# Phase tables as matrix products in the set-up of an FFT-and-feed-forward kernel, with the first batch folded in two halves

## The chip, the cores and the metric

The kernel runs on one core of one Trainium2 chip. The core has five engines with queues of their own: TensorE (PE; its weight loads are listed as PEld), VectorE (DVE), ScalarE (ACT), GpSimd (POOL) and SyncE (SP). The metric is device time in microseconds of one execution, and the median of several runs is compared. The profile is one execution taken by the hardware profiler. All times inside it are counted from the start of its span.

## The reference

The input x has 8 batches of 3008 rows of 256 numbers. A Fourier transform runs over both axes of each batch and its real part is kept. Every row of 256 then goes through a feed-forward layer with a squared ReLU.

```python
X = np.fft.fft(np.fft.fft(x, axis=1), axis=2).real      # 8 x 3008 x 256
h = np.maximum(X.reshape(24064, 256) @ w_in, 0.0)       # w_in 256 x 2048
out = h * h @ w_out                                     # w_out 2048 x 256
```

## The kernel before

All heavy work is matmuls in 16 bits with sums in 32 bits. The transform is done by products with cosine and sine tables, and symmetry makes the products small. A row of x and its mirror image are added and subtracted ("folded"), along the 256 columns (`fe`, `fo`) and then along the 3008 rows (`ab`). The result is split again into odd and even output frequencies. For the odd class the folded tile is `od`, with part 0 for cosines and part 1 for sines; its tables are `cos0` and `sin0`, six rows of 376 frequencies for each of the 128 partitions.

`z_steps` (L468) multiplies `od` with the tables. Each unit has parts 0 and 1 and halves h = 0 and 1, of three matmuls each (L488) into a PSUM tile `pz`. After half 0, ACT copies the partial sum to `es` (L493); after half 1, ACT copies the sum into the window's columns `zc` or `zs` (L497); the step `minus` (L504, on DVE) forms the mirrored columns as 2 es - ps.

The transform along the columns is merged into the input weights. `gh_step` (L440) multiplies the tables `c_all` and `s_n` with a quarter of w_in (512 of 2048 columns) in PSUM, and its `scale` step writes the quarter into `gh`, rows 0 and 1, by ACT or DVE. `gh_turn` (L456) makes row 2 from row 1 with the factors `turn2`. So for each window of z columns the hidden values are gh[0] times zc plus gh[1] times zs; adding gh[2] times zs then gives those of the mirrored columns.

The loop over windows w (L697) makes the hidden values, squares them into `h2`, and multiplies the h2 of the window before with the output weights `wout16` (L628). Windows 0 and 1 have 240 and 512 columns. Window 0 takes two groups of four steps: `pq4` (eight matmuls, L834 and L835), `square4` (ACT's relu L844, DVE's square L847), `turn4` (four matmuls, L840), and `square4` again. `others(s)` issues what is planned beside step s. Window 1 carries the fold of the second batch (`x1`), with DVE work in `d_even`, `n_cos`, `d_odd`, `n_sin` and `odds`, then `nyq`, two tiny matmuls on PE (L383, L384) and a DVE copy (L385).

The order on each engine is the order in which the program issues it; no scheduler reorders it. DMAs of the inputs are issued by POOL. `load_x` (L124 on) loads a batch in one direct transfer (L133: the first two quarters of the rows) and two gathers through index vectors (L138: the mirrored quarters). The order on POOL is: iotas `nvec_i`, `irow_i`, `dvec_i`, `idx_r`; load of the first batch; iota `prow_i` and two permutation matrices `perm`; two small index vectors; the two halves of w_in (`w16`, L185); w_out (L187). The load of the second batch is issued in `d_odd` and waits for the DVE instruction that last reads the first batch.

The odd tables are made by `table_steps(0)`. The phase n times k modulo 3008 comes out of elementwise work: six ACT instructions `args` (L240) that round n k / 3008 to a whole number, `turns` (L246) and `mods` (L252) on DVE, then two sines over 1128 columns (L258). Row 1 gets a weight (L279). The cosines are the sines of mirrored rows, fetched by matmuls with the permutations (L268) and copied by ACT (L269). The tables for the columns are made in a like way on ACT and DVE (L294 to L322). `idle(n)` (L308) issues n matmuls of 384 columns on zeros, whose results nobody reads.

PSUM pools: `ps_h`, two tiles of 2 x 512; `ps_o` and `ps_z`, two tiles of 512 each. `h1p` has five tiles, used in turn by the relus.

Of the kernel before, what the change touches and what calls it, by code (L numbers as in the profile page):

```python
# [15 lines left out]
P = 128  # L16
# [12 lines left out]
def kernel(  # L29
# [94 lines left out]
    def load_x(i):  # L124
# [18 lines left out]

        if b > 0:
            direct(0, 2)
        else:
# [5 lines left out]
        gather(2, idx["r" if b + 1 < B else "c"][:, 0:1], o + (S - R * (P - 1)) * D)  # L152
# [5 lines left out]
        gather(3, idx["r"][:, 0:1], o + (H - R * (P - 1)) * D)  # L158
        return t

    def iota(shape, pattern, base, mult, name):
        t = const.tile(shape, I32, name=name)
        nc.gpsimd.iota(t, pattern=pattern, base=base, channel_multiplier=mult)
        return t
# [3 lines left out]
    nvec_i = iota([P, R], [[1, R]], -5, R, "nvec_i")  # L168
    irow_i = iota([P, NE], [[1, NE]], 0, 0, "irow_i")
    dvec_i = iota([P, 2], [[P, 2]], 0, 1, "dvec_i")  # L170
# [6 lines left out]
    for i in (1, 0):  # L177
        nc.gpsimd.tensor_scalar(out=perm[i], in0=prow_i, scalar1=float(P - 1 - i), scalar2=None, op0=ALU.is_equal)
# [5 lines left out]
    for i in range(2):  # L184
        nc.gpsimd.dma_start(out=w16[i], in_=moe_w_in[:, i * F // 2 : (i + 1) * F // 2].rearrange("(c p) f -> p c f", p=P))  # L185
    wout16 = const.tile([P, NFC, D], F16, name="wout16")
# [9 lines left out]
    nraw = small([P, R], "nraw")  # L196
    nc.vector.tensor_copy(nraw, nvec_i)
    irow = small([P, NE], "irow")
    nc.vector.tensor_copy(irow, irow_i)

    nvec = small([P, R], "nvec")
    nc.vector.scalar_tensor_tensor(out=nvec, in0=nraw, scalar=float(Q), in1=nraw, op0=ALU.is_le, op1=ALU.mult)
    nc.vector.tensor_scalar(out=nvec, in0=nvec, scalar1=0.0, scalar2=None, op0=ALU.max)
    nvs = small([P, R], "nvs")
    nc.vector.tensor_scalar(out=nvs, in0=nvec, scalar1=1.0 / S, scalar2=None, op0=ALU.mult)

    wgt = small([P, 1], "wgt")
    nc.vector.tensor_scalar(out=wgt, in0=nraw[:, 1:2], scalar1=float(Q), scalar2=-0.5, op0=ALU.is_equal, op1=ALU.mult)
# [4 lines left out]
    def table_steps(e):  # L213

        n = unit_cols[e][0]
        nr = 2 if e else 3
        cos_t = const.tile([P, 2 if e else R, n], F16, name=f"cos{e}")
        sin_t = const.tile([P, 2 if e else R, n], F16, name=f"sin{e}")
        tabs[e] = (cos_t, sin_t)
        vec, vs = (evec, evs) if e else (nvec, nvs)  # L220
        st = {}

        def row(h, j):
            return j if e else RQ[3 * h + j]

        def freq():
            kf = st["kf"] = tmp.tile([P, NE], F32, name="kf", tag="kf")[:, 0:n]
            i = 0
            for k0, kstep, cnt in unit_runs[e][0]:
                nc.vector.tensor_scalar(out=kf[:, i : i + cnt], in0=irow[:, i : i + cnt], scalar1=float(kstep), scalar2=float(k0 - kstep * i), op0=ALU.mult, op1=ALU.add)  # L230
                i += cnt

        def args(h):
            tm = tmp.tile([P, 2, 3, NE], F32, name="tm", tag="tt")
            t, st["m", h] = tm[:, 0], tm[:, 1]
            st["t", h] = t
            for j in range(nr):
                r = row(h, j)
                if e == 0:
                    nc.scalar.activation(t[:, j, 0:n], st["kf"], AF.Copy, bias=R23, scale=vs[:, r : r + 1])  # L240
                else:
                    nc.vector.tensor_scalar(out=t[:, j, 0:n], in0=st["kf"], scalar1=vs[:, r : r + 1], scalar2=R23, op0=ALU.mult, op1=ALU.add)
# [5 lines left out]
        def mods(h):  # L248
            m = st["m", h]
            for j in range(nr):  # L250
                r = row(h, j)
                nc.vector.scalar_tensor_tensor(out=m[:, j, 0:n], in0=st["kf"], scalar=vec[:, r : r + 1], in1=st["t", h][:, j, 0:n], op0=ALU.mult, op1=ALU.add)  # L252
# [4 lines left out]
        def sins(h):  # L257
            nc.scalar.activation(sin_t[:, 3 * h : 3 * h + nr, :], st["m", h][:, 0:nr, 0:n], AF.Sin, bias=0.0, scale=wk)  # L258

        def coss(h):  # L260
            if e:
                nc.scalar.activation(cos_t, st["t", h][:, 0:nr, 0:n], AF.Sin, bias=halfpi[:, 0:1], scale=-wk)
                return

            pc = ps_h.tile([P, 2, 512], F32, name="pc", tag="psh")
            for j in range(2):
                r = RQ[2 * h + j]
                nc.tensor.matmul(pc[:, j, 0:n], perm[1 if r else 0], sin_t[:, RQ.index(6 - r if r else 0), :], start=True, stop=True)  # L268
            nc.scalar.activation(cos_t[:, 2 * h : 2 * h + 2, :], pc[:, :, 0:n], AF.Copy, bias=0.0, scale=1.0)  # L269

        def weigh():
            if e:
                for t in (cos_t, sin_t):
                    for r in range(2):
                        nc.vector.tensor_scalar(out=t[:, r, :], in0=t[:, r, :], scalar1=wge[:, r : r + 1], scalar2=None, op0=ALU.mult)
                return

            q = RQ.index(1)
            nc.scalar.activation(sin_t[:, q, :], sin_t[:, q, :], AF.Copy, bias=0.0, scale=wgt)  # L279
# [3 lines left out]
    to = table_steps(0)  # L283
    to["freq"]()

    dvec = small([P, 2], "dvec")
    nc.vector.tensor_copy(dvec, dvec_i)
    dvs = small([P, 2], "dvs")
    nc.vector.tensor_scalar(out=dvs, in0=dvec, scalar1=1.0 / D, scalar2=None, op0=ALU.mult)
    drow = irow[:, 0 : P + 1]  # L290
    am = h1p.tile([P, 2, P + 1], F32, name="am", tag="h1")
    at = h1p.tile([P, 2, P + 1], F32, name="at", tag="h1")
    for c in range(2):
        nc.scalar.activation(at[:, c, :], drow, AF.Copy, bias=R23, scale=dvs[:, c : c + 1])  # L294
    nc.vector.tensor_scalar(out=at, in0=at, scalar1=-R23, scalar2=-float(D), op0=ALU.add, op1=ALU.mult)
    for c in range(2):
        nc.vector.scalar_tensor_tensor(out=am[:, c, :], in0=drow, scalar=dvec[:, c : c + 1], in1=at[:, c, :], op0=ALU.mult, op1=ALU.add)
# [7 lines left out]
    nc.vector.memset(fe.rearrange("p q c d -> p (q c) d")[:, :, 129:130], 0.0)  # L305
    pw = ps_o.tile([P, 512], F32, name="pw", tag="po")
# [6 lines left out]
    idle(16)  # L313
    to["args"](0)
    to["args"](1)
    wd = 2.0 * math.pi / D
    s_n = const.tile([P, 2, P + 1], F16, name="s_n")
    nc.scalar.activation(s_n, am, AF.Sin, bias=0.0, scale=-wd)
    nc.vector.tensor_scalar(out=at.bitcast(I32), in0=am.bitcast(I32), scalar1=0x7FFFFFFF, scalar2=None, op0=ALU.bitwise_and)
    c_all = const.tile([P, 2, P + 1], F16, name="c_all")  # L320
    nc.scalar.activation(c_all, at, AF.Sin, bias=halfpi[:, 0:1], scale=-wd)
    nc.scalar.activation(s_n[:, :, 0:1], c_all[:, :, P : P + 1], AF.Copy, bias=0.0, scale=0.5)  # L322

    to["turns"](0)
    to["mods"](0)
    to["sins"](0)
    to["turns"](1)
    to["weigh"]()
    idle(4)
    to["coss"](0)  # L330
    to["mods"](1)
    to["sins"](1)
    idle(6)
    to["coss"](1)
    to["coss"](2)
    idle(4)

    turn2 = small([P, 1], "turn2")
    nc.vector.tensor_scalar(out=turn2, in0=dvec[:, 0:1], scalar1=0.0, scalar2=2.0, op0=ALU.is_equal, op1=ALU.mult)
    nc.vector.tensor_scalar(out=turn2, in0=turn2, scalar1=-2.0, scalar2=None, op0=ALU.add)  # L340
# [3 lines left out]
    def fold_steps(i):  # L344
# [7 lines left out]
        lo = xf[:, :, 1:129]  # L352
        hi = rev_dim(xf[:, :, 128:256], 2)
# [3 lines left out]
        def d_even():  # L357
            nc.vector.tensor_copy(t[0:1, 2, 0, :], t[0:1, 0, R - 1, :])
            nc.vector.tensor_tensor(fef[:, :, 1:129], lo, hi, op=ALU.add)
            nc.vector.tensor_copy(fef[:, :, 0:1], xf[:, :, 0:1])  # L360

        def d_odd():
            nc.vector.tensor_tensor(fof[:, :, 1:129], lo, hi, op=ALU.subtract)
            if i + 1 < B:
                xs[i + 1] = load_x(i + 1)

        def n_cos():
            nc.vector.tensor_tensor(ab[:, 0], fe[:, 0:2], rev_dim(fe[:, 2:4], 2), op=ALU.add)

        def n_sin():  # L370
            nc.vector.tensor_tensor(ab[:, 1], fo[:, 0:2], rev_dim(fo[:, 2:4], 2), op=ALU.subtract)
# [566 lines left out]
```

## Time and profile before

| What | us |
|---|---|
| median of 3 runs | 603.11 (601.97 to 604.74) |
| profiled execution, its own time | 604.8 |
| its span | 603.0 |
| mean granted TensorE clock | 0.997 of full |
| first matmul of window 0 (L834) | 23.40 |
| first relu of window 0 (L844) | 24.94 |
| first matmul of window 1 (L748) | 31.45 |
| fold of the second batch starts on DVE (L358) | 35.09 |

The profile's pages list for each engine how long it was busy, what ended its idle time, and the chain of work that ended last. A row of the timeline gives start, length, engine, line, operation, output and inputs, and in brackets the idle time ahead of it and what ended it. A count such as x6 is several like instructions merged in one row.

### The profile page before, as it was taken

How to read it: one execution, taken by the hardware profiler on the slowest of the kernel's cores; microseconds unless marked ns; L12 is line 12 of the kernel's file. 1: busy time of each engine (PE TensorE's matmuls, PEld its weight loads, DVE VectorE, ACT ScalarE, POOL GpSimd, SP SyncE). 2: the span in 40 equal slices, each digit the busy share in tenths (PEclk: the TensorE clock that was granted, in tenths of full speed). 3: DMA queues.
4: the chain of work that ended last, by engine and by line, in shares of the span. 5: the costliest groups of instructions: out<-in, count | busy, mean ns of one | idle time of the engine just before them, and what ended most of it. 6: DMA issues, size and time to landing. Idle time of an engine off the chain costs nothing.

```text
span 603.0 us, 11343 instructions
## 1 busy us (share of the span) xinstructions
PE 580.4 (96%) x4376; PEld 421.1 (70%) x4376; DVE 515.0 (85%) x740; ACT 515.4 (85%) x663; POOL 88.7 (15%) x125
## 2 busy tenths in 40 slices
PE   5899999999999999999999999999999999999997
PEld 2557776777677677777677766766777776776786
DVE  7797677887999988989989899888998699889981
ACT  7596788888999889989899898979989888888972
POOL 5353200103001032020012200401000020000000
PEclk9899999999999999999999999999999999999999
DMA  8937120273213533542154311643112231211222
GB/s 143 205 85 161 56 71 31 63 154 92 68 45 72 135 113 70 128 116 56 51 111 91 111 45 54 116 111 90 48 33 71 71 89 46 61 43 48 60 59 68
DMA packets 39736, 50.33 MB, mean 83 GB/s; under 512 B 4589, under 2 KB 33539, under 8 KB 39683
## 3 DMA queue, kind: packets, MB, share of 16 engines
q0 software_dynamic: 9344, 22.14, 18.6%
q1 hardware_dynamic: 26899, 24.44, 13.8%
q10 hardware_dynamic: 3440, 3.03, 2.1%
q8 instruction: 34, 0.56, 0.4%
q14 instruction: 19, 0.16, 0.1%
HBM read 36.42 MB, written 27.86 MB: 107 GB/s over the span
## 4 chain that ended last, share of the span: by engine, by line
PE 66%; ACT 12%; DVE 10%; issue 5%; DMA 4%; POOL 1%; ACTq 0%; SPq 0%; DVEq 0%; POOLq 0%
PE po L628 39%; PE ph L787 5%; PE ph L773 5%; PE ph L754 4%; PE ph L748 4%; ACT h L758 4%; PE ph L749 4%; PE pz L488 3%; ACT sn L781 3%; DMA out_dram<-osb 2%; ACT osb L643 2%; DVE h L813 2%; ACT hd L789 2%; DVE hd L812 2%; DVE hd L811 1%
## 5 line engine op out<-in xcount | busy, mean ns | idle before, releaser
L628 PE MATMUL po<-wout,h 128*128 128x256 f16 (+1 forms) x3024 | 362.0, 273 | 1.3 <-DVE h L813 1.3
L628 PEld LDWEIGHTS <-h 128*128 128x128 f16 (+1 forms) x3024 | 296.4, 98 | 73.0 <-DVE h L813 1.8
L758 ACT ACTIVATE h<-ph 128x1024 f16<-128x1024 f32 (+3 forms) x196 | 185.6, 981 | 13.8 <-PE ph L754 8.3
L763 DVE TENSOR_TENSOR h<-h 128x1024 f16<-128x1024 f16 (+3 forms) x135 | 85.3, 657 | 26.5 <-ACT h L758 25.2
L789 ACT ACTIVATE hd<-ph 128x1024 f16<-128x1024 f32 (+3 forms) x94 | 94.0, 1001 | 14.9 <-PE ph L787 13.4
L813 DVE TENSOR_TENSOR h<-hd 128x4096 f16<-128x4096 f16 (+6 forms) x51 | 105.4, 2066 | 1.4
L781 ACT ACTIVATE sn<-ph 128x1024 f16<-128x1024 f32 (+3 forms) x94 | 93.6, 996 | 1.0 <-PE ph L773 0.7
L643 ACT ACTIVATE osb<-po 128x512 f32<-128x512 f32 (+3 forms) x95 | 54.6, 578 | 24.8 <-PE po L628 24.0
L748 PE MATMUL ph<-zc,gh 128*128 128x512 f16 (+3 forms) x196 | 72.1, 368 | 0.5 <-ACT h L844 0.3
L749 PE MATMUL ph<-zs,gh 128*128 128x512 f16 (+3 forms) x196 | 72.1, 368 | 0.0
L797 DVE TENSOR_SCALAR hd<-eb,wv 128x512 f16<-128x512 f16 (+3 forms) x188 | 54.2, 348 | 15.1 <-DMA eb<-zr 15.1
L801 DVE TENSOR_TENSOR sn<-sn,hd 128x2048 f16<-128x2048 f16 (+6 forms) x51 | 56.7, 1113 | 11.8 <-ACT sn L781 8.1
L811 DVE TENSOR_TENSOR hd<-hd,sn 128x2048 f16<-128x2048 f16 (+6 forms) x51 | 56.6, 1111 | 9.8 <-ACT hd L789 8.4
L761 ACT ACTIVATE h<-h 128x1024 f16<-128x1024 f16 (+3 forms) x61 | 62.7, 1028 | 1.9
L787 PE MATMUL ph<-zc,gh 128*128 128x512 f16 (+3 forms) x188 | 54.6, 371 | 5.7 <-ACT sn L781 4.7
L812 DVE TENSOR_SCALAR hd<-hd 128x4096 f16<-128x4096 f16 (+6 forms) x51 | 56.8, 1114 | 1.5
L754 PE MATMUL ph<-zs,gh 128*128 128x512 f16 (+3 forms) x196 | 55.3, 368 | 0.2 <-ACT h L758 0.2
L773 PE MATMUL ph<-zs,gh 128*128 128x512 f16 (+3 forms) x188 | 54.5, 372 | 0.0
L749 PEld LDWEIGHTS <-gh 128*128 128x128 f16 x196 | 19.1, 98 | 21.2 <-issue 1.0
L748 PEld LDWEIGHTS <-gh 128*128 128x128 f16 x196 | 19.1, 97 | 20.3
L773 PEld LDWEIGHTS <-gh 128*128 128x128 f16 x188 | 18.3, 97 | 20.9
L787 PEld LDWEIGHTS <-gh 128*128 128x128 f16 x188 | 17.1, 97 | 13.7 <-issue 9.5
(129 smaller groups left out, 408.2 us busy)
## 6 DMA issues: line engine op xcount, KB each, us to landing
out_dram<-osb SPq DMA_DIRECT2D x77, 128.0 KB
xo<-in_x_dram POOLq DMA_DIRECT2D x7, 768.0 KB, 7.0
scr<-ev POOLq DMA_DIRECT2D x8, 390.0 KB, 5.0
eb<-zr ACTq DMA_DIRECT2D x19, 128.0 KB
rb<-scr POOLq DMA_DIRECT2D x16, 130.0 KB, 2.4
out_dram<-osb SPq DMA_DIRECT2D x12, 94.0 KB
w<-in_moe_w_in_dram POOLq DMA_DIRECT2D x2, 512.0 KB, 9.5
wout<-in_moe_w_out_dram POOLq DMA_DIRECT2D x1, 1024.0 KB, 14.8
```

Source lines behind the costliest of these rows:

```text
L628: nc.tensor.matmul(po[0:m, j * D : (j + 1) * D], h2[:, fc, q : q + m], wout16[:, fc, :], start=(fc == 0 and (j == 0 or not four or i > 3)) ...
L748: nc.tensor.matmul(ph[:, a, 0:wn], gh[:, 0, f0 : f0 + P], zcw[:, 0:wn], start=True, stop=False)
L749: nc.tensor.matmul(ph[:, a, 0:wn], gh[:, 1, f0 : f0 + P], zsw[:, 0:wn], start=False, stop=True)
L754: nc.tensor.matmul(phs[s][:, a, 0:wn], gh[:, 2, f0 : f0 + P], zsw[:, 0:wn], start=False, stop=True, skip_group_check=True)
L758: nc.scalar.activation(h1[:, :, 0:wn], phs[s][:, :, 0:wn], AF.Relu)
L763: return [lambda: nc.vector.tensor_tensor(h2[:, 2 * s : 2 * s + 2, sg * wn : (sg + 1) * wn], hv, hv, op=ALU.mult)]
L773: nc.tensor.matmul(ph[:, a, 0:wn], gh[:, 1, f0 : f0 + P], zsw[:, 0:wn], start=True, stop=True)
L781: nc.scalar.activation(sns[g][:, i : i + 2, 0:wn], ph[:, :, 0:wn], AF.Copy, bias=0.0, scale=-2.0)
L787: nc.tensor.matmul(ph[:, a, 0:wn], gh[:, 0, f0 : f0 + P], zcw[:, 0:wn], start=False, stop=True, skip_group_check=True)
L789: nc.scalar.activation(hds[g][:, i : i + 2, 0:wn], ph[:, :, 0:wn], AF.Copy, bias=0.0, scale=1.0)
L812: lambda: nc.vector.tensor_scalar(out=hv, in0=hv, scalar1=0.0, scalar2=None, op0=ALU.max),
L813: lambda: nc.vector.tensor_tensor(h2[:, 2 * g[0] : 2 * g[-1] + 2, 0 : 2 * wn], hv, hv, op=ALU.mult),
```

## The change

- POOL issues the first batch's direct transfer ahead of all iotas. `load_x` is a generator now, so that the gathers follow behind the iotas they need.
- The odd tables' phases come from PE. With one row of numbers n and one row of frequencies k, a matmul with a single contraction row gives n k in PSUM; a second adds 1536 x 3008. ACT divides by 3008 into 16 bits, which rounds to a whole number; a matmul with a diagonal matrix of -3008 subtracts that many turns in the same PSUM tile, and ACT's sine reads the PSUM tile. Two of six rows are handled at a time (a[0], a[1], a[2]). The column tables are made likewise (d), the cosine with a quarter turn added.
- The numbers n, k and others are iotas in 16 bits in three `h1p` tiles. The permutations and the two diagonal matrices are made by DVE. The 30 idle matmuls become 24 here, and 4 more stand between the first two parts of z.
- The fold of the first batch runs in two halves, hf = 0 (first direct quarter and first gather) and hf = 1. Each makes its half of fe, ab's cosine part, fo and ab's sine part.
- z's parts 0,0 and 0,1 come ahead of the first weight product. The second quarter of gh is scaled by DVE; the third is made in two halves in `ps_o`; the fourth inside window 0, between the two `turn4` of its first group, one half scaled by DVE and one by ACT.
- z's two `minus` steps move from ahead of window 0 into its step 0.

```diff
+    x0 = load_x(0)
+    next(x0)
...
+    line(nrow, [[1, R], [R, P]], 1 - R)
+    line(krow, [[4, E]], 1)
+    line(jp[:, P : 2 * P], [[1, P]], 0, -1)
     idx["r"] = iota([P, 1], [[1, 1]], P - 1, -1, "idx_r")
-    xs = {0: load_x(0)}
-    prow_i = iota([P, P], [[1, P]], 0, 1, "prow_i")
+    xs = {0: next(x0)}
+    line(jp[:, 0:P], [[1, P]], 0, 1)
+    line(fcol, [[1, P + 1]])
+    line(drw, [[1, 2 * P]])
+    dvec = iota([P, 1], [[1, 1]], 0, 1, "dvec", F32)
...
+    def phase_n(g):
+        pv = ps_h.tile([P, 2, 512], F32, name="pv", tag="psh")
+        for j in range(2):
+            nc.tensor.matmul(pv[:, j, 0:E], nrow[:, RQ[2 * g + j], :], krow, start=True, stop=False)
+            nc.tensor.matmul(pv[:, j, 0:E], hun, ncol, start=False, stop=True)
...
+    def whole(v, t, dg, m, *to):
+        nc.scalar.activation(t, v, AF.Copy, bias=0.0, scale=1.0 / m)
+    def rest(v, t, dg, m, *to):
+        for j in range(2):
+            nc.tensor.matmul(v[:, j], dg, t[:, j], start=False, stop=True, skip_group_check=True)
+    def sine(v, t, dg, m, to, w):
+        nc.scalar.activation(to, v, AF.Sin, bias=0.0, scale=w)
+    a = [phase_n(0), phase_n(1)]
+    whole(*a[0])
+    rest(*a[0])
+    whole(*a[1])
+    rest(*a[1])
+    d = [phase_d(0), phase_d(1)]
+    sine(*a[0])
+    a.append(phase_n(2))
+    sine(*a[1])
+    whole(*a[2])
+    rest(*a[2])
+    for t in d:
+        whole(*t)
+        rest(*t)
+    sine(*a[2])
...
-    idle(16)
-    to["args"](0)
-    to["args"](1)
...
+    for g in range(3):
+        pc = ps_h.tile([P, 2, 512], F32, name="pc", tag="psh")
+        for j in range(2):
+            r = RQ[2 * g + j]
+            nc.tensor.matmul(pc[:, j, 0:E], perm[1 if r else 0], sin_o[:, RQ.index(6 - r if r else 0), :], start=True, stop=True)
+        nc.scalar.activation(cos_o[:, 2 * g : 2 * g + 2, :], pc[:, :, 0:E], AF.Copy, bias=0.0, scale=1.0)
+        if g == 0:
+            for t in d:
+                sine(*t)
+            nc.scalar.activation(s_n[:, :, 0:1], c_all[:, :, P : P + 1], AF.Copy, bias=0.0, scale=0.5)
+        idle(6)
     idle(6)
...
-    run(f0s["d_even"], f0s["n_cos"], lambda: f0s["odd"](0))
+    for hf in range(2):
+        f0s["d_even"](hf)
+        f0s["n_cos"](hf)
+        if hf:
+            f0s["odd"](0)
+        f0s["d_odd"](hf)
+        f0s["n_sin"](hf)
+    f0s["odd"](1)
+    run(*z0(0, 0))
+    idle(4)
+    run(*z0(0, 1))
     gh_step(0, True)()
-    run(*z0(0, 0))
-    run(f0s["d_odd"])
-    gh_step(1, True)()
-    run(*z0(0, 1))
-    gh2 = gh_step(2, False)
-    run(f0s["n_sin"], lambda: f0s["odd"](1), f0s["nyq"], gh2)
+    f0s["nyq"]()
     run(*z0(1, 0))
-    gh3 = gh_step(3, False)
+    gh1 = gh_step(1, False)
     gh_turn(0)
-    gh3()
+    gh1()
+    gh_turn(1)
     run(*z0(1, 1))
-    run(*z0(0, 2))
-    run(*z0(1, 2))
+    for i in range(2):
+        gh_half(2, i, False)()
+    gh_turn(2)
...
+            at[0] = [lambda: run(*z0(0, 2)), lambda: run(*z0(1, 2))]
...
-                for s in ss:
-                    turn4(s)
-                for s in ss:
-                    square4(s, 1)
+                turn4(s0)
+                gh3 = [gh_half(3, i, i == 1) for i in range(2)] if s0 == 0 else []
+                turn4(s0 + 2)
+                run(*gh3[0:1])
+                square4(s0, 1)
+                run(*gh3[1:])
+                square4(s0 + 2, 1)
+                if s0 == 0:
+                    gh_turn(3)
```

`gh_half(cc, i, act)` is `gh_step` for one of the two tables: two matmuls of 512 columns into a `ps_o` tile and one scaling instruction.

More of the change, by code (lines that the diff above doesn't have):

```diff
@@ L185 @@
         nc.gpsimd.dma_start(out=w16[i], in_=moe_w_in[:, i * F // 2 : (i + 1) * F // 2].rearrange("(c p) f -> p c f", p=P))
+    irow = iota([P, NE], [[1, NE]], 0, 0, "irow", F32)
     wout16 = const.tile([P, NFC, D], F16, name="wout16")
@@ L211, with table_steps @@
     wk = 2.0 * math.pi / S
[L213 to L220, printed above, removed]
+    for e in range(2):
+        tabs[e] = [const.tile([P, 2 if e else R, unit_cols[e][0]], F16, name=f"{f}{e}") for f in ("cos", "sin")]
+    def table_steps():
+        n, nr = NE, 2
+        cos_t, sin_t = tabs[1]
         st = {}
-        def row(h, j):
-            return j if e else RQ[3 * h + j]
         def freq():
@@ L233, in args @@
         def args(h):
-            tm = tmp.tile([P, 2, 3, NE], F32, name="tm", tag="tt")
+            tm = tmp.tile([P, 2, nr, NE], F32, name="tm", tag="tt")
             t, st["m", h] = tm[:, 0], tm[:, 1]
             st["t", h] = t
[L237 to L242, printed above, removed]
+            for r in range(nr):
+                nc.vector.tensor_scalar(out=t[:, r, 0:n], in0=st["kf"], scalar1=evs[:, r : r + 1], scalar2=R23, op0=ALU.mult, op1=ALU.add)
         def turns(h):
@@ L249, in mods @@
             m = st["m", h]
-            for j in range(nr):
-                r = row(h, j)
-                nc.vector.scalar_tensor_tensor(out=m[:, j, 0:n], in0=st["kf"], scalar=vec[:, r : r + 1], in1=st["t", h][:, j, 0:n], op0=ALU.mult, op1=ALU.add)
+            for r in range(nr):
+                nc.vector.scalar_tensor_tensor(out=m[:, r, 0:n], in0=st["kf"], scalar=evec[:, r : r + 1], in1=st["t", h][:, r, 0:n], op0=ALU.mult, op1=ALU.add)
         def absm(h):
@@ L257, in sins @@
         def sins(h):
-            nc.scalar.activation(sin_t[:, 3 * h : 3 * h + nr, :], st["m", h][:, 0:nr, 0:n], AF.Sin, bias=0.0, scale=wk)
+            nc.scalar.activation(sin_t, st["m", h][:, 0:nr, 0:n], AF.Sin, bias=0.0, scale=wk)
         def coss(h):
[L261 to L268, printed above, removed]
@@ L293 @@
[L293 to L297, printed above, removed]
+            nc.scalar.activation(cos_t, st["t", h][:, 0:nr, 0:n], AF.Sin, bias=halfpi[:, 0:1], scale=-wk)
+        def weigh():
+            for t in (cos_t, sin_t):
+                for r in range(2):
+                    nc.vector.tensor_scalar(out=t[:, r, :], in0=t[:, r, :], scalar1=wge[:, r : r + 1], scalar2=None, op0=ALU.mult)
@@ L311, in idle @@
             nc.tensor.matmul(pw[:, 0 : 3 * P], spn[:, 0, 0, :], spn.rearrange("p c r d -> p (c r d)")[:, 0 : 3 * P], start=True, stop=True)
-    idle(16)
-    to["args"](0)
-    to["args"](1)
[L316 to L332, printed above, removed]
-    idle(6)
[L334 to L340, printed above, removed]
+    q = RQ.index(1)
+    nc.scalar.activation(sin_o[:, q, :], sin_o[:, q, :], AF.Copy, bias=0.0, scale=wgt)
+    for g in range(3):
[9 more added lines that the diff above has]
+        idle(6)
+    idle(6)
     folded = {}
@@ L452, in scale, with gh_half @@
                 nc.vector.tensor_scalar(out=gh[:, 0:2, f0 : f0 + 512], in0=pg, scalar1=1.0 / HS, scalar2=None, op0=ALU.mult)
+        return scale
+    def gh_half(cc, i, act):
+        f0 = cc * 512
+        fw = f0 % (F // 2)
+        pg = ps_o.tile([P, 512], F32, name="pg", tag="po")
+        for c in range(2):
+            nc.tensor.matmul(pg, (c_all, s_n)[i][:, c, 0:P], w16[f0 // (F // 2)][:, c, fw : fw + 512], start=(c == 0), stop=(c == 1))
+        def scale():
+            if act:
+                nc.scalar.activation(gh[:, i, f0 : f0 + 512], pg, AF.Copy, bias=0.0, scale=1.0 / HS)
+            else:
+                nc.vector.tensor_scalar(out=gh[:, i, f0 : f0 + 512], in0=pg, scalar1=1.0 / HS, scalar2=None, op0=ALU.mult)
         return scale
@@ L567 @@
     nc.gpsimd.tensor_tensor(wge, wge, wg2, op=ALU.add)
-    for cc in range(1, F // 512):
-        gh_turn(cc)
     wv = small([P, NFC], "wv")
```

129 lines of the change are left out of this document (75 added, 54 removed).

## The prediction

> **What bounds the kernel now.** I read the busy shares first, then the set-up in the timeline and in the chain of waits, then the clock in short windows. From 30 us on TensorE (PE) is busy nearly all the time, so what the set-up loses or gains there comes out at the end: a matmul of window 1 that starts 1 us earlier ends the run 1 us earlier, unless a wait appears. The page, then stretches of the table by windows (busy time of PE, PEld, DVE, ACT, POOL, then granted clock, DMA share, GB/s):
>
> ```profile
> PE 580.4 (96%) x4376; PEld 421.1 (70%) x4376; DVE 515.0 (85%) x740; ACT 515.4 (85%) x663; POOL 88.7 (15%) x125
> ```
>
> ```profile
> 0.00:5.00 5.00, 0.00 (x0) 0.00 (x0) 3.12 (x15) 3.30 (x7) 3.74 (x11) 1.00 0.37 50
> ...
> 15.85:24.00 8.15, 7.53 (x31) 3.45 (x32) 5.59 (x7) 3.77 (x8) 4.58 (x11) 0.79 1.34 205
> 24.00:30.00 6.00, 4.96 (x42) 4.04 (x42) 5.40 (x12) 5.00 (x7) 0.00 (x0) 1.00 1.06 210
> ...
> 45.00:60.00 15.00, 14.71 (x123) 10.88 (x124) 11.78 (x25) 10.76 (x17) 5.25 (x3) 1.00 0.77 164
> ```
>
> The chain of waits in order of time (start, length, what) names the gate of the set-up: the first half of the input weights, w, on DMA, then PE with weight products (L446) and mixing matmuls (L488) by turns, then ACT's relus of window 0 (L844).
>
> ```profile
> 7.15 8.66 DMA w<-in_moe_w_in_dram
> 15.85 1.79 PE pg L446 x4
> 17.65 0.94 PE pz L488 x3
> 18.59 1.32 PE pg L446 x4
> ...
> 24.94 2.70 ACT h L844 x3
> ```
>
> The timeline shows what stands beside that chain:
>
> ```profile
> 12.26 1.79 DVE L359 TENSOR_TENSOR fe<-xo 128x3072 f16<-128x3072 f16 x1 [1.15 <-DMA xo<-in_x_dram,idx_r]
> 13.14 1.49 ACT L269 ACTIVATE cos<-pc 128x752 f16<-128x752 f32 x2 [0.41 <-PE pc L268]
> 15.69 1.78 DVE L363 TENSOR_TENSOR fo<-xo 128x3072 f16<-128x3072 f16 x1
> 15.85 0.94 PE L446 MATMUL pg<-w,c_all 128*128 128x512 f16 x2 [1.78 <-DMA w<-in_moe_w_in_dram]
> 24.94 3.56 ACT L844 ACTIVATE h<-ph 128x960 f16<-128x960 f32 x4 [0.79 <-PE ph L835]
> 31.45 0.38 PE L748 MATMUL ph<-zc,gh 128*128 128x512 f16 x1 [0.29 <-ACT h L844]
> ```
>
> The odd tables end at 14.63, the first half of od at 15.78 (15.21 + 0.57), w at 15.81; PE has by then stood for 1.78 us, and runs at half clock in the rows that follow:
>
> ```profile
> 16.00:17.00 1.00, 1.00 (x3) 0.30 (x2) 1.00 (x1) 0.00 (x0) 0.00 (x0) 0.50 1.15 217
> 18.00:19.00 1.00, 1.00 (x4) 0.45 (x3) 0.97 (x2) 1.00 (x2) 0.70 (x2) 0.50 1.46 200
> ```
>
> About 3.4 us at half clock, so some 1.7 us of PE's own work lost on the chain.
>
> **The change, part by part.** Times below are from the span's start. All engines start at about 0.75.
>
> *POOL and the load.* The direct load of the first batch goes ahead of the iotas: it starts at 0.75 in place of 1.49, so the transfers, which follow without a gap from about 4.5 to 30 us (some 210 GB/s), come 0.7 us earlier. The last gather, which now ends DVE's wait at 12.26, lands at 11.55, w at 15.1; the first half of the batch (direct and first gather, 1.18 of 1.57 MB) 0.39 MB / 0.21 = 1.9 us before the whole, 9.6. The gathers' issues are moved behind three wider iotas. Rows: 0.13 us for 6 elements, 0.45 for 377; so 0.8 for 768, 0.45 for 376, 0.26 for 128, 0.13 for idx_r, which brings the gathers from 2.74 to about 3.4 to 3.7 and the last to 4.7 to 5.1. Cover: the direct load's 0.79 MB moves until about 6.9. If the 16-bit iotas cost twice the 32-bit rows, PE's first matmul, which needs two of them, is 1.2 us later; below the row I see no reason for a gain. I take the row. w, wout and x1 follow on POOL as before, SP's queue is not passed by anything, and irow's iota (0.45) goes ahead of wout, which is not read before 33.
>
> *Tables.* DVE loses two turns (1.0 each), six products (0.6 each), kf, the casts and am: about 8 us of work, and is free when the batch lands; it gains memsets and four 128x128 comparisons of 0.1 to 0.2, done by 7.5. ACT loses six args (3.09) and the two 1128-wide sines and gets, for three pairs of rows, a rounding copy and a sine of 752 columns each (row L269: 0.80, start to start 0.69) and two copies of 258 (0.40). PE gets 12 one-row products and 6 corrections of 376, and 14 of 129. The chain: nrow and krow at 3.0; PE is cold (row L311: 384 columns take 0.32 from 5.19 to about 9.1, 0.16 after), so four products 1.25 + 0.15 drain; copy at 4.5, correction behind the second pair, second copy 5.7, sines at 6.4 and 7.1. The third pair needs the PSUM of the first sine and stands behind the 129-column products: on PE 7.9 to 8.7; copy to 9.5, two copies to 10.1, sine 10.0 to 10.8, weighting 0.6, first cosine copy to 12.2, s_n, c_all and its column (0.9) to 13.0, two cosine copies to 14.5. So the odd tables end at 14.5 against 14.63: no gain by itself.
>
> *PE's filler.* 24 idle matmuls of 384 columns (30 before) stand between the cosine products: first product 10.3, six at 0.16, second 11.65, six, third 12.95, then twelve. At full clock PE is through at 15.2; that, not the tables, starts z.
>
> *Fold in halves.* Each half costs half of the whole's rows (1.79, 0.96) plus the fixed part of about 0.1: copy from 9.6, then 0.85 + 0.12 + 0.48 + 0.85 + 0.48 to 12.6; second half with od's part 0 at 14.65 (15.78 before), all at 16.5 (19.08). If the halves cost as much as wholes, which no row shows, od's part 0 comes 1.3 later and moves z by 1.2; between the ends I take the half, since 1560 elements (0.96) cost about half of 3072 (1.79).
>
> *Weight products.* They stand behind z, so PE does not wait for w: the 1.78 us of standing go, and so does what follows them, the half clock. From z at 15.2 PE has 12 mixing matmuls of 0.157 (1.88), 12 weight products of 0.215 (2.58), 4 idle (0.65), and 0.81 + 0.15 for window 0's first eight; add 0.4 for nyq's way over DVE and 0.3 for the wait for zs: 6.8. First relu at 22.0 (24.94 before).
>
> *Window 0.* Before, 24.94 to 31.45 is 6.51, eight ACT steps of 0.89. It now holds the last quarter of the weight products too: PE 4 x 0.215, ACT one copy of 512 columns (row L450 halved: 0.55), DVE 0.65 + 0.3, and the two subtractions for z (0.54 each) come inside. ACT's share is on the path: 6.51 + 0.55 = 7.1, and 0.2 for turn4(2), now behind gh3's matmuls. Window 1 starts at 22.0 + 7.3 = 29.3, 2.1 us earlier. DVE's extra 2 us end 0.6 us later against window 1's start than before; they lie under its first square, which DVE gets 2.1 us after that start (33.56 - 31.45). Without that cover PE's 0.39 us wait for od at 45.2 becomes 1.0. Next batch: x1's issue, queued on POOL behind DVE's fo, goes earlier too, and x1 is not read before 33.
>
> *Sum.* Window 1's start 31.45 - 2.1 = 29.3. Against the profiled execution (span 603.0, 604.8 with what lies around it) 602.7; against the median of 603.11, which is 1.7 below it, **601.0**. That the other two runs of before (603.11, 601.97) stand lower by the size of the half-clock stretch may mean that they did not have it; then less of the gain is left.
>
> In the trace the clock opens 3.9 us after the first filler matmul (5.19 to about 9.1), and after 1.78 us of standing, with 0.78 shortly before, it is at 0.50. The Trainium skill (TensorE: Matmul & The Clock Gate, part 1) has the clock watched over free-running windows of 3.4 us, so one kernel can open it at different moments, and (Why this matters for your kernels) allows gaps of up to about 3 us; in the second the trace differs. By the row PE is warm here at 6.9 and window 1 starts at 29.2; by the page between 6.4 and 9.8, and window 1, as an estimate, between 29.0 and 30.6.
>
> **Rivals.**
> 1. *More than 3 us.* Clock open by 5.7 (PE is busy from 3.0) and no loss in window 0: the table chain ends 0.8 earlier, window 1 at 28.8, and od, done earlier, ends the 0.39 wait at 45.2: 3.0 to 3.2 us, **599.9**. For it: before's half-clock stretch is in the trace, all gaps of PE after 10 us are under 0.3 us in my chain. Against: ACT's chain of 12 steps bounds it.
> 2. *Slower: PE cold at z.* One-row products and PE's waits for ACT (up to 0.9 at 9) may not open the clock; only the filler from 10.3 does, after 3.9 us, 14.2. The 12 idle matmuls, z's predecessors in PE's order, then end at 18.6 and window 1 starts at about 32.2; with a second closing like that at 15.97 (1.7) 33.9: 2.4 us slower, **605.5**. It decides from the point where PE is cold past 13. Against: before opened it after 3.9 us of plain filler.
> 3. *Hidden anyway.* The tables gate as before and before's median had no half-clock stretch: without it window 1 before starts 1.5 to 1.7 earlier, and 0.4 to 0.6 of the gain is left: **602.6**.
>
> **How the numbers follow.** Forecast 0.40, rival 1 0.34, rival 2 0.16, rival 3 0.10. About 0.5% (3.0 us) is what a measurement of this kernel can tell from no change. Rival 1 stands just past that bound and the forecast 0.9 us short of it; the runs of before scatter by -1.1 to +1.6 us about their median. So faster takes four fifths of rival 1 and three tenths of the forecast, 0.39, given as 0.40; slower the half of rival 2 that scatter carries past 606.1, 0.08; within 0.5% the rest, 0.52. The range: 599.9 less 1.1 is 598.8; 602.6 with the doubled iotas' 1.2 and the late clock in part gives 605.0, short of rival 2's upper half.
>
> **What would show it.** Right: a clock of 1.00 from about 7 to the end and no 0.50 rows between 10 and 22; od's part 0 near 14.7; z's first matmul near 15.2 with PE, not DVE, ahead of it; first relu of window 0 near 22.0, window 1 near 29.3. Wrong: idle matmuls of 0.32 after 11 us (rival 2); the cosine copies past 15.5; PE waiting for od or for w ahead of z; a DVE wait over 0.5 ahead of window 1's nyq; iotas over 1 us each.

## The result and the profile after

Measured by turns on one chip, 12 runs each, the kernel before took 603.58 us (601.97 to 606.40) and the changed kernel 605.74 (605.14 to 606.72). The ratio is 1.0032, with a 95% interval of 1.0018 to 1.0046: slower by about a third of a per cent. The profiled execution of the changed kernel took 606.72 of its own, its span is 605.0.

| us | before | after | forecast |
|---|---|---|---|
| clock first full | 9.16 | 16.96 | 6.9 |
| odd tables end | 14.63 | 18.46 | 14.5 |
| `od`, part 0, ends | 15.78 | 16.08 | 14.65 |
| first matmul of z | 17.44 | 19.41 | 15.2 |
| first relu of window 0 | 24.94 | 26.15 | 22.0 |
| first matmul of window 1 | 31.45 | 33.15 | 29.3 |
| span | 603.0 | 605.0 | 603.0 - 2.1 = 600.9 |

The clock's row comes from the trace's own records of the clock, which begin at its first change. The views of the profile show 1.00 where there is no record yet, so ahead of the first change the clock has to be read from the spacing of the rows. The span less the start of window 1 is 571.55 before and 571.85 after: from window 1 on nothing was won or lost beyond 0.3 us, and the rest of the difference between the two profiled executions lies in the set-up.

The busy shares of the page after:

```profile
PE 585.7 (97%) x4406; PEld 424.3 (70%) x4406; DVE 510.9 (84%) x739; ACT 514.2 (85%) x661; POOL 82.4 (14%) x127
```

PE has 5.3 us more of busy time than before and DVE 4.1 less. The elementwise work did leave DVE, and that bought nothing. The chain of waits says who sets the end now (start, length, what):

```profile
10.35 0.81 ACT ti L321
...
11.20 1.22 PE pv L325 x6
12.41 0.63 PE pc L359 x2
13.04 1.92 PE pw L350 x6
14.96 0.63 PE pc L359 x2
15.59 1.72 PE pw L350 x6
17.30 0.32 PE pc L359 x2
17.62 1.95 PE pw L350 x12
19.57 0.48 PE pz L538 x3
...
26.15 1.65 ACT h L900 x2
```

The transfer of w, 8.66 us of the chain before, is gone from it. In its place stand the idle matmuls, `pw`: 1.92 + 1.72 + 1.95 = 5.6 us of filler ahead of z, the last twelve of them its direct predecessors. Six of them take 1.92, which is 0.32 each, half speed; the twelve behind 17.62 take 0.16 each. The timeline shows the phase products ahead of them (start, length, engine, line, operation, operands):

```profile
3.54 0.46 PE L305 MATMUL pv<-rows 1*128 1x376 f16 x1 [3.54 <-POOL rows L183]
3.80 0.51 PE L306 MATMUL pv<-rows 1*128 1x376 f16 x1
4.11 0.51 PE L305 MATMUL pv<-rows 1*128 1x376 f16 x1
...
9.48 0.52 PE L305 MATMUL pv<-rows 1*128 1x376 f16 x1
9.79 0.52 PE L306 MATMUL pv<-rows 1*128 1x376 f16 x1
...
11.20 0.78 PE L325 MATMUL pv<-ti,dg 128*128 128x376 f16 x2 [0.89 <-ACT ti L321]
...
12.83 2.12 PE L350 MATMUL pw<-spn 128*128 128x384 f16 x6
...
15.62 0.80 ACT L360 ACTIVATE cos<-pc 128x752 f16<-128x752 f32 x1 [0.83 <-PE pc L359]
...
17.66 0.80 ACT L360 ACTIVATE cos<-pc 128x752 f16<-128x752 f32 x1 [1.24 <-PE pc L359]
19.41 0.64 PE L538 MATMUL pz<-cos,od 128*128 128x376 f16 x3
```

The phase products follow each other every 0.31 us at 4 us and still every 0.31 us at 9.5, after nearly six microseconds in which PE shows hardly a gap (by the windows it was busy for 1.85 of 2 us from 6 to 8 and 2.00 of 2 from 8 to 10). The clock does not open there. It opens 4.1 us behind the first idle matmul, and 5.8 us behind the corrections of full height at 11.20, from which on PE has no gap. ACT waits 0.83 and 1.24 for cosine products that stand behind half-speed filler.

### The profile page after: what moved, and what is told of

Read it like the earlier page. It is cut to its first block, busy times and chain, and to the rows that moved or that the text cites. A ratio compares the mean times of both kernels' runs of the same rounds, so it can differ in the third digit from the quotient of the medians.

```text
span 605.0 us, 11404 instructions
## 1 busy us (share of the span) xinstructions
PE 585.7 (97%) x4406; PEld 424.3 (70%) x4406; DVE 510.9 (84%) x739; ACT 514.2 (85%) x661; POOL 82.4 (14%) x127
## 4 chain that ended last, share of the span: by engine, by line
PE 66%; ACT 14%; DVE 9%; issue 5%; DMA 4%; POOL 0%; ACTq 0%; SPq 0%; DVEq 0%; POOLq 0%
PE po L683 37%; PE ph L843 5%; ACT h L814 5%; PE ph L829 4%; PE ph L804 4%; PE ph L810 4%; PE ph L805 4%; DMA out_dram<-osb 3%; PE pz L538 3%; ACT sn L837 3%; ACT osb L698 2%; ACT hd L845 2%; DVE h L869 1%; DVE hd L868 1%; DVE hd L867 1%
```

## The experiments

The theory (A): a product of one contraction row does not count for what opens the clock. So PE stays at half speed until full-height matmuls have run for some time, the filler runs at 0.32 each, and z, which stands behind it in PE's order, comes late. Against it stand: (B) the gaps of PE, where it waits for ACT, keep the clock shut; (C) the price is the filler alone, whatever the clock; (D) the fold in halves and the new order of the weight products are what costs. "Opens" is the first full clock in the trace, z and window 1 are first matmuls, all in us from the start of the span; z and window 1 are those of the profiled execution.

| run | median (range) | ratio to before | opens | z | window 1 |
|---|---|---|---|---|---|
| padded | 603.18 (602.89 to 603.58) | 0.9984 [0.9971, 0.9997] | 8.21 | 16.12 | 29.88 |
| gaps | 605.86 (605.30 to 606.85) | 1.0031 [1.0018, 1.0044] | 13.48 | 17.87 | 31.62 |
| nofiller | 604.82 (603.35 to 608.61) | 1.0017 [0.9999, 1.0035] | 19.93 | 16.12 | 31.37 |
| oldtables | 603.59 (603.21 to 605.84) | 1.0000 [0.9985, 1.0015] | 11.19 | 16.54 | 30.30 |
| cosfirst_onerow | 605.75 (604.74 to 607.95) | 1.0034 [1.0020, 1.0049] | 16.24 | 19.05 | 32.80 |
| cosfirst | 601.90 (601.54 to 602.18) | 0.9963 [0.9942, 0.9984] | 7.22 | 14.65 | 28.75 |
| combined | 602.21 (601.69 to 602.61) | 0.9977 [0.9964, 0.9989] | 9.56 | 14.94 | 29.20 |
| beforefill | 603.51 (602.77 to 603.77) | 0.9988 [0.9970, 1.0005] | 9.14 | 16.78 | 30.12 |
| rows32 | 606.28 (one run) | none | 16.76 | 19.35 | 33.10 |
| rows8 | 605.35 (one run) | none | 15.13 | 18.55 | 32.30 |

The first four ran on one chip, where before had a median of 603.83 (602.54 to 606.10, 35 runs), the next four on another, where it had 603.37 (602.23 to 609.33; 35 runs). rows32 and rows8 ran once each on a third, where the one run of before took 608.70: of these two only the clock and the rows are read, not the time.

### padded: the phase products over 128 rows, 127 of them zero

```diff
-            nc.tensor.matmul(pv[:, j, 0:E], nrow[:, RQ[2 * g + j], :], krow, start=True, stop=False)
-            nc.tensor.matmul(pv[:, j, 0:E], hun, ncol, start=False, stop=True)
+            nc.tensor.matmul(pv[:, j, 0:E], nrow_f[:, RQ[2 * g + j], :], krow_f, start=True, stop=False)
+            nc.tensor.matmul(pv[:, j, 0:E], hun_f, ncol_f, start=False, stop=True)
```

The three tiles of rows are cleared first, and the products of the column tables are widened likewise.

> The changed kernel with its one-row products (phases n k) made over all 128 rows, 127 of them zeros; the tiles are set to zero first. Same columns, same order, same results. Theory A (matmuls that use one row of the array do not count for the clock gate): the clock opens at 7 to 10 us in place of 17.0, the filler runs at 0.16 a piece, window 1 starts at 29.3 to 30.5 (33.15 in the changed kernel), the run takes 602 to 603. Theory B (the waits of 0.3 to 1.2 us that PE has for ACT between 6 and 11.2 us hold the clock back, whatever the rows): still half clock until about 17, window 1 at 33.0 to 33.5, 605.5 to 606.

The timeline of this run:

```profile
4.51 0.52 PE L309 MATMUL pv<-rows 128*128 128x376 f16 x1
4.83 0.52 PE L308 MATMUL pv<-rows 128*128 128x376 f16 x1
...
8.71 0.32 PE L309 MATMUL pv<-rows 128*128 128x376 f16 x1
8.87 0.32 PE L308 MATMUL pv<-rows 128*128 128x376 f16 x1
...
13.81 2.11 PE L353 MATMUL pw<-spn 128*128 128x384 f16 x12
...
15.49 0.57 DVE L413 TENSOR_TENSOR od<-ab 128x774 f16<-128x774 f16 x1
...
16.12 0.65 PE L541 MATMUL pz<-cos,od 128*128 128x376 f16 x3 [0.20 <-DVE od L413]
```

A cold product of 128 rows takes as long from start to start as one of a single row (0.32 from 4.51 to 4.83, 0.31 from 3.80 to 4.11 in the changed kernel), so padding costs PE no time. But the clock opens at 8.21, and from there the spacing is 0.16. The last twelve idle matmuls are through at 15.92, and z then waits for `od`, no longer for PE. That is theory A. It also speaks against C: the filler is the same here, and with the clock open it holds up nothing. The added rows are zeros, and so are all rows of the idle matmuls, which open the clock too: what counts is how many rows a product has, not what they hold. Both operands of each product were padded together, so whether the weights or the moving rows count is not told apart. Window 1 comes 3.27 us earlier than in the changed kernel; the medians differ by 2.56, since the profiled execution of the changed kernel (606.72) is the longest of its twelve.

### gaps: filler put into PE's waits for ACT, the products left at one row

```diff
+    idle(1)
     d = [phase_d(0), phase_d(1)]
...
+    idle(3)
     for t in d:
```

> The changed kernel with filler matmuls over 128 rows put into PE's waits for ACT: one behind the second correction, three behind the third pair's products (all clock-cold, 0.32 each). The one-row products stay as they are. Theory A (one row does not count): the windows of the gate up to 10 us still hold mostly one-row work, the clock opens at 13.5 or later, at the earliest one window of 3.4 us ahead of the changed kernel's 17.0; window 1 at 32 to 33.3. Theory B (the waits): the clock opens at 7 to 10.2, window 1 at 29.3 to 30.7, the run takes 602 to 603.

The timeline of this run has filler where the changed kernel's PE waited from 10.3 to 11.2:

```profile
10.12 0.52 PE L306 MATMUL pv<-rows 1*128 1x376 f16 x1
10.57 1.14 PE L335 MATMUL pw<-spn 128*128 128x384 f16 x3
...
12.56 0.83 PE L361 MATMUL pc<-sin,perm 128*128 128x376 f16 x2
13.19 1.29 PE L335 MATMUL pw<-spn 128*128 128x384 f16 x6
```

PE is busy without a break from 7.66, and the clock still opens only at 13.48, 2.9 us behind the first filler at 10.57. The median is that of the changed kernel. Theory B falls as the main cause. What the four matmuls won between the two profiled executions, 1.5 us of window 1, the medians do not show: this one (605.30) is the shortest of its twelve, that of the changed kernel the longest.

### nofiller: the 28 idle matmuls left out

```diff
-        idle(6)
-    idle(6)
...
-    idle(4)
```

> The changed kernel without its 28 idle matmuls. By either theory the clock is shut then up to z and beyond; the question is what the filler itself costs when it runs at half clock ahead of z in PE's order. In the changed kernel the last cosine copy would be ready at about 16 without the 18 filler matmuls ahead of it and od's part 0 is ready at 16.08. If the filler's 24 slow pieces are the price: z's first matmul at 16.1 to 16.5 in place of 19.41, but its matmuls and the weight products at half clock for 3.4 us or more: window 1 at 31.5 to 32.5, the run 604 to 605. If the warm clock that the filler buys is worth as much as it costs: window 1 at 33 or later, 605.5 or more.

```profile
16.12 1.12 PE L536 MATMUL pz<-cos,od 128*128 128x376 f16 x3 [1.29 <-DVE od L408]
...
18.70 1.06 PE L479 MATMUL pg<-w,c_all 128*128 128x512 f16 x2
```

Now z starts at 16.12 behind `od`, but at half speed: 1.12 us for three matmuls against 0.65, and 1.06 for two weight products against 0.59. The clock opens at 19.93. By the medians the filler costs the changed kernel 0.9 us net (605.74 against 604.82), and 1.6 of the 2.6 us between it and padded stay without any filler. But these kernels were not measured side by side, and against before the ratios are 1.0032 and 1.0017 with intervals that overlap: how the price divides between the filler and the cold clock at z is not settled.

### oldtables: the tables and the load of before, with the fold in halves and the new order

The cut is against the changed kernel.

```diff
-    x0 = load_x(0)
-    next(x0)
...
+    xs = {0: load_x(0)}
...
-    a = [phase_n(0), phase_n(1)]
...
+    to = table_steps(0)
+    to["freq"]()
```

> The kernel before with the change's other half: fold in two halves, z ahead of the weight products, the last products inside window 0; tables, iotas and load as before. If the tables by PE with their cold clock are the whole loss: the clock opens at 9.1 as before, od's part 0 at about 16.1, z then at 16.1, window 1 at 30.2 to 31.0 if the stand of PE from 14.1 to 16 does not shut the clock, 31.7 to 32.5 if it does; 602 to 604.5. If the reordering itself loses (0.55 of ACT and 0.86 of PE in window 0, the folds' fixed parts): window 1 at 32.5 or later, slower than 605.

```profile
16.54 0.65 PE L512 MATMUL pz<-cos,od 128*128 128x376 f16 x3 [1.46 <-DVE od L384]
```

A ratio of 1.0000, with an interval of 0.0015 (0.9 us) to either side: the fold in halves and the new order do not cost the 0.32% of the changed kernel, so D falls, and they win nothing that shows either. PE no longer stands for w, but it stands for `od`: z starts at 16.54 behind part 0, which ends at 16.48 (15.78 before), since in halves the first half's sine work stands ahead of it on DVE. The clock opened at 11.19, not at 9.1 as expected, although the filler starts as in before; the last cosine products start at 13.79 (12.78 before), and z waits for `od` all the same.

### rows32 and rows8: how high must a product be?

The kernel padded, with 32 or 8 rows in all in place of 128. One row only of each pair of operands is not zero, as in padded.

```diff
-    krow_f = rows[1][:, 0:E]
+    krow_f = rows[1][0:32, 0:E]
```

> As padded (zero rows added to the phase products), but 32 rows in all in place of 128. If the clock gate weighs a matmul by the rows that it uses, a quarter of the array doesn't open it: the clock opens past 13 and window 1 starts past 31.5. If only products of a single row are not counted, or it takes few rows, the clock opens by 10.5, z starts by 16.5 and window 1 by 30.3, as in padded (8.21, 16.12, 29.88).

> As padded, but 8 rows in all. Weighing by rows: clock past 13, window 1 past 31.5, whatever 32 rows did. Only single rows not counted: clock by 10.5, window 1 by 30.3. If 32 rows open it and 8 don't, a threshold lies between.

The timeline of rows32:

```profile
4.20 0.51 PE L308 MATMUL pv<-rows 32*128 32x376 f16 x1
4.52 0.51 PE L309 MATMUL pv<-rows 32*128 32x376 f16 x1
...
12.92 2.12 PE L353 MATMUL pw<-spn 128*128 128x384 f16 x6
...
19.35 0.64 PE L541 MATMUL pz<-cos,od 128*128 128x376 f16 x3
```

In this run thirty-two rows do no more for the clock than one: it opens at 16.76, and z comes at 19.35. So it is no peculiarity of single rows. Openings fall into two groups without overlap: 7.22, 8.21 and 9.56 in the three kernels with 128 rows, 13.48 to 16.96 in the five that have 1, 8 or 32 rows and their filler. Whether the rows are weighed in proportion, or a threshold lies between 32 and 128, is left open.

The Trainium skill (TensorE: Matmul & The Clock Gate, part 1) has the clock follow how busy PE was, over free-running windows of 3.4 us. The windows agree with the scatter within a group: some 2.3 us between three kernels with the same products, and 2.0 between before, beforefill and oldtables, whose filler starts at 5.19 or 5.20 in each and whose clock opens at 9.16, 9.14 and 11.19. "Busy", as the profile counts it, does not: PE was busy for 6.61 of the 6.76 us from 3.54 to 10.30 in the changed kernel, and for 6.82 of 6.97 from 3.53 to 10.50 in gaps, and the clock stayed shut; in padded it opened after 4.33 of 4.59 (3.62 to 8.21).

### cosfirst_onerow and cosfirst: DVE makes the cosine halves first

In padded z waits for `od`, part 0. On DVE the sine work of the first half (`fo`, `ab`) stands ahead of it; here it goes behind.

```diff
     for hf in range(2):
         f0s["d_even"](hf)
         f0s["n_cos"](hf)
-        if hf:
-            f0s["odd"](0)
-        f0s["d_odd"](hf)
-        f0s["n_sin"](hf)
-    f0s["odd"](1)
+    f0s["odd"](0)
+    run(f0s["d_odd"], f0s["n_sin"], lambda: f0s["odd"](1))
```

With one-row products:

> The changed kernel with only DVE's order of the first fold changed: both cosine halves and od's part 0 first, then the sine parts whole. Products of one row and all filler stay. If the late z of the changed kernel is PE's cold filler alone, as the padded run says, od's part 0 comes at about 14.4 in place of 16.08 and nothing follows from it: z still at 18.5 to 19.5 behind the filler, window 1 at 32.5 to 33.3, 605 to 606. If od's late part 0 has a share in it, the run falls by 1 us or more, to 604.7 or below.

With 128 rows, and 9 idle matmuls fewer:

> The padded kernel (products over 128 rows) with the same new order of the first fold on DVE, and 9 idle matmuls fewer behind the last cosine product, since z shall start earlier. In the padded kernel z waited for DVE (od's part 0 at 16.07, z at 16.12). If DVE's order is the gate there: od's part 0 at 14.4, z at 14.5 to 15.0; nyq's way then waits for od's part 1 at about 17.7, so of the 1.4 us at z only 0 to 0.5 reach window 1 (29.88 in the padded kernel). The run takes 602.6 to 603.2.

The timeline of cosfirst:

```profile
13.34 0.65 PE L353 MATMUL pw<-spn 128*128 128x384 f16 x3
14.65 0.65 PE L540 MATMUL pz<-cos,od 128*128 128x376 f16 x3 [0.66 <-DVE od L412]
...
28.75 0.38 PE L803 MATMUL ph<-zc,gh 128*128 128x512 f16 x1 [0.29 <-ACT h L899]
```

With one-row products DVE ends `od`, part 0, at 14.68, and z comes only at 19.05, behind the filler. The same order is worth nothing there (605.75) and, with the nine idle matmuls fewer that let z follow, another 1.3 us behind the warm filler (603.18 to 601.90; not side by side, but by the ratios to before as well). A gate can be judged only when the one in front of it is gone. cosfirst beats both kernels: 0.9963 [0.9942, 0.9984], and its longest run (602.18) is below the shortest of the changed kernel. It gained more than was expected of it. z moved as foreseen, by 1.47 us from 16.12 to 14.65, but window 1 came 1.13 us earlier in place of 0.5 at most. The second gate, od's part 1, was where it was expected (its last copy starts on DVE at 17.80); only z's sine part, which PE's order held until 19.17 in padded, could still move to 18.04 before it met that gate.

### combined: cosfirst with three more moves

The iota `irow` goes behind the issue of wout, the second quarter of the weight products ahead of `nyq`, the third ahead of z's last part.

```diff
+    gh1 = gh_step(1, False)
     f0s["nyq"]()
...
-    gh1 = gh_step(1, False)
...
+    gh2 = [gh_half(2, i, False) for i in range(2)]
     run(*z0(1, 1))
```

> The one before with two more moves: irow's iota behind the issue of w_out on POOL (the fold's first copy took 0.45 to 0.66 us in place of 0.21 while POOL issued w_out), and the second quarter's weight products ahead of nyq, the third's ahead of the last part of z, so that PE works while it waits for od's part 1. The copy then ends 0.2 to 0.4 earlier; z at 14.2 to 14.7; first relu of window 0 at 21.2 to 22.0 (22.88 in the padded kernel), window 1 at 28.2 to 29.0, the run 601.5 to 602.4, faster than both kernels. If the copy's length has another cause than POOL's issue it stays at 0.45 or more.

No gain: 602.21 against 601.90 beside it. The timeline has two reasons:

```profile
13.16 1.14 PE L353 MATMUL pw<-spn 128*128 128x384 f16 x6
...
18.38 0.17 PE L421 MATMUL py<-od,perm 128*128 128x5 f16 x1
18.83 0.65 PE L540 MATMUL pz<-sin,od 128*128 128x376 f16 x3 [0.28 <-DVE od L422]
```

The tiny products of `nyq` now stand behind eight weight products and are ready at 18.38 where cosfirst had them at 17.24, and z's sine part, which waits for them, starts at 18.83 against 18.04. And in this execution, the longest of its twelve, the clock opened at 9.56, the filler came 1.1 us later than in cosfirst (the second six at 13.16 against 12.04), and z at 14.94 behind it, with no wait for `od`. The two are not told apart here. What moving the iota did to the fold's first copy stands in the last section.

### beforefill: before, with idle(14) for the last idle(4)

It fills the 1.78 us in which PE stood for w, so that the clock does not close at 16.

```diff
-    idle(4)
+    idle(14)
```

> The kernel before with 14 idle matmuls in place of 4 behind the last cosine product, which fill PE's stand of 1.78 us ahead of w. If the half-clock stretch that this stand brought in the profiled execution costs many executions 1.7 us: no half clock between 10 and 22 us, window 1 at 29.8 to 30.3 (31.45 before), median 602.0 to 603.0, and a smaller scatter than that of before (602.54 to 606.1). If the stretch was a matter of that one execution: 603.5 to 604.0 as before.

The windows of this run (busy time of PE, PEld, DVE, ACT, POOL, then granted clock, DMA share, GB/s):

```profile
14.00:16.00 2.00, 1.78 (x12) 0.88 (x10) 1.93 (x5) 0.61 (x1) 0.00 (x0) 1.00 1.06 180
16.00:17.00 1.00, 1.00 (x6) 0.47 (x6) 1.00 (x1) 0.02 (x1) 0.00 (x0) 1.00 1.11 211
```

The half clock from 16 is gone. The median is that of before (603.51 against 603.37, ratio 0.9988 [0.9970, 1.0005]), but the scatter shrinks to 1.0 us, from 602.77 to 603.77, where before reached up to 609.33. So the typical execution of before lost next to nothing to the half clock; the profiled one, 604.8 at a mean granted clock of 0.997, is one of those that did. The runs of before divide by that clock: beside beforefill 13 of 35 had 0.997 or less, and a median of 604.66, the other 22 one of 602.78. The ten idle matmuls thus do away with the long executions and leave the others no faster: beforefill's 603.51 is 0.7 above the 602.78, for a reason that no run shows. Nor does every such stand close the clock: in oldtables PE stood for 0.79 and 1.46 us at about the same place, and the trace has 1.00 behind it.

## Why the prediction was wrong

**The step that failed** is the one on the clock: "by the row PE is warm here at 6.9". It took the 3.9 us from the first filler matmul of before and laid it on the one-row products. The row was that of matmuls of full height; nothing in the trace of before showed a low one, so the term had no row behind it. The runs put 16.96 in place of 6.9. With it fell "At full clock PE is through at 15.2; that, not the tables, starts z": the first two sixes of filler ran at 0.32 or nearly so, and z came at 19.41. That PE's order, not the tables, starts z was right.

**The rival that came true** is the second, "Slower: PE cold at z". Of its two conditions the runs show the one on the one-row products, not the one on PE's waits; its place and its deciding point are those of the trace (the clock opened past 13). That 605.5 lies so near the measured 605.74 is in part luck. The 605.5 holds a second closing of 1.7 us (window 1 at 33.9), and the trace has none: the clock is 1.00 from 16.96 on. And it counts from 31.45, the start of window 1 in an execution of before that had lost time to a half clock, as most had not; the two errors nearly cancel. Without the second closing the rival put window 1 at 32.2; the profiled execution has 33.15, but stands 1.0 above its median, so 32.2 is right for a typical one, as an estimate. Its clock, 14.2, was early, because it let the filler begin at 10.3; PE's first product came at 3.54 in place of 3.0, and at half speed the chain of the third pair brings the first cosine product to 12.21. What was put against it, that before opened its clock after 3.9 us of plain filler, speaks of the filler and not of the products, and was no ground for a chance as small as 0.16.

**The load and the fold.** The direct transfer was to be issued at 0.75; it was issued at 1.27, since POOL's queue stood until then. Before it was 1.5, so 0.2 us were won in place of 0.7. The first half of the batch ended DVE's wait at 10.05 (9.6 forecast); the copy of one row behind it took 0.66 for 0.21, and the halves about half a microsecond more than I gave them. So `od`, part 0, ended at 16.08 and not at 14.65. This did not decide the changed kernel, but it would have decided the forecast: padded has its clock open well ahead of z (8.21) and has z at 16.12 in place of 15.2, window 1 at 29.88 in place of 29.3, and 0.65 us on the median in place of 2.1.

**The baseline.** The sum was made against a profiled execution that held a half-clock stretch; its 1.7 us were counted as a gain of the change. beforefill, and the clocks of the runs beside it, show that the median of before does not hold them. The third rival had said this with a chance of 0.10: as an estimate by the medians, window 1 of before starts near 31.45 - (604.8 - 603.58) = 30.2, that of padded near 30.0. So the new order, right in its mechanism (PE no longer waits for w, and no 0.50 stands between 10 and 22 once the clock is open), had no half clock to win back in a typical execution, and its stand for w of 1.78 us became one of 1.46 for `od`: it is worth nothing in oldtables.

**What held.** From z's first matmul to the first relu 6.8 us were forecast and 6.74 measured; for window 0 7.3 and 7.0. The cover in window 1 held: PE's wait for `od` is 0.43 at 46.95, it was 0.39. What window 1 starts later comes out at the end, within 0.3 us; over all runs the span less its start is 571.0 to 571.9. The tables' chain, 14.5 forecast and 18.46 measured, was right in its steps and wrong by its clock: its last cosine copy stands behind filler, and padded, with the clock open, had the third pair of cosine products start at 13.49 and the last copy end at 14.88.

## What to carry to other kernels

A matmul can keep PE busy in the profile and still not bring up its clock: where a warm-up rests on products with few contraction rows, pad the operands to full height with zero rows, which cost PE no time here, and read the clock from the spacing of equal rows. Filler is a bet on the clock; at half speed every idle matmul delays what stands behind it in PE's order twice as much (0.32 us against 0.16 here). Before a gain is worked out from one profiled execution, see whether the median holds the stall that is to be removed.

## What the runs showed of the hardware

The clock and the height of products is above. The other surprise is the copy of one row of 256 elements ahead of the fold, 0.21 us before, when POOL was through with its issue of wout at 9.96:

```profile
8.78 1.18 POOL L187 DMA_DIRECT2D wout<-in_moe_w_out_dram  x1
10.90 0.21 DVE L358 COPY xo<-xo 1x256 f16<-1x256 f16 x1
```

In the changed kernel it took 0.66; the timeline has it beside POOL's issue of wout:

```profile
9.47 1.19 POOL L206 DMA_DIRECT2D wout<-in_moe_w_out_dram  x1
10.05 0.66 DVE L388 COPY xo<-xo 1x256 f16<-1x256 f16 x1 [1.79 <-DMA xo<-in_x_dram,idx_r]
```

In cosfirst it starts later and takes 0.38:

```profile
9.47 1.19 POOL L209 DMA_DIRECT2D wout<-in_moe_w_out_dram  x1
10.33 0.38 DVE L390 COPY xo<-xo 1x256 f16<-1x256 f16 x1 [2.07 <-DMA xo<-in_x_dram,idx_r]
```

In combined the issue is over by then, and an iota is in its place:

```profile
10.22 0.50 POOL L168 IOTA irow<- 128x377 f32 x1
10.24 0.56 DVE L390 COPY xo<-xo 1x256 f16<-1x256 f16 x1 [1.99 <-DMA xo<-in_x_dram,idx_r]
```

Whatever its start, the copy ends within 0.1 us behind POOL's instruction: 10.71 after 10.66, again 10.71 after 10.66, 10.80 after 10.72. The other six kernels with the load of the changed one agree (the copy ends at 10.69 to 10.71, the issue at 10.65 to 10.68), and in oldtables, with the load of before, it takes 0.21. So moving the iota behind the issue could not free it. The Trainium skill (SBUF — State Buffer, "Who interferes with whom") tells of a port pair that DVE and GpSimd share as an exclusive lock: a DVE copy can take it in its two-port modes, and whoever issues first holds it for the whole instruction. These ends agree with that. In which mode the copy ran no run shows, and that the lock is the cause was not tried alone.
